# A fused H3 and MLP kernel: background work issued by an estimate of VectorE's open work instead of a fixed pace

## The chip, the cores and the metric

One core of a Trainium2 chip runs the whole program in one launch. The metric is the device time of one execution in microseconds (us). The engines are TensorE (PE in the profile, its weight loads PEld), VectorE (DVE), ScalarE (ACT), GpSimd (POOL) and SyncE (SP), which issues the DMAs.

## The reference

Two layers, each an H3 operator followed by an MLP with squared relu, on one sequence of 2048 tokens with 1024 channels; F is 3584.

```python
def _A_ref(q, k, v, shift_k, ssm_k, ssm_D):          # H3
    k_shift = sum of k_pad[:, t:t+S] * shift_k[:, 3-t]   # causal convolution over 4 tokens
    kv = k_shift * v
    y = causal convolution of kv with ssm_k over all S tokens, by channel   # written with FFTs
    return q * (y + kv * ssm_D)

def _B_ref(x, w1, b1, w2, b2):                       # MLP
    h = relu(x @ w1 + b1)
    return (h * h) @ w2 + b2

x = A_q
x = x + _A_ref(_layernorm(x), A_k, A_v, A_shift_k, A_ssm_k, A_ssm_D)
x = x + _B_ref(_layernorm(x), B_w1, B_b1, B_w2, B_b2)
x = x + _A_ref(_layernorm(x), A_k, A_v, A_shift_k, A_ssm_k, A_ssm_D)
x = x + _B_ref(_layernorm(x), B_w1, B_b1, B_w2, B_b2)
```

The convolution does not depend on the layer: the same y serves both. All arithmetic is as exact as float32: each matmul is three matmuls, of the high and low halves of its operands.

## The kernel before, in words

**Units and steps.** The tokens are four blocks of 512. A unit is one layer's MLP on one block, and `ORDER` gives the eight units: layer and block (0,0), (1,0), (0,1), (0,2), (1,1), (0,3), (1,2), (1,3). A unit is a list of steps. A step is twelve matmuls of 512 columns with one weight tile of 128 x 512: `m1` multiplies by w1, `m2` by w2. A full unit has 112 steps. Around the passage from the first unit to the second, which share a block, steps are halved (256 columns or two of four token tiles). With these the first unit has 134 steps, the second 124, the others 112: the last steps of units 0 to 4 have the numbers 133, 257, 369, 481 and 593. The loop over the steps writes the instructions of all engines in one order; each engine then runs its own in order and waits on semaphores.

**Weights.** Each weight tile is loaded (`w_load`), its high half is cast on ScalarE (`w_hi`, L770) and its low half made on VectorE (`w_lo`, L778: `whl`). In the first unit all tiles pass this way, and about two thirds are stored as pairs (`w_store`, L786, `wd_m`) and loaded ready-made in later units (`whl<-wd_m`, L768). The results of `m1` pass relu and square on ScalarE (L1141 to L1144) and give `rh`, and `rl` on VectorE (L1149). VectorE adds the results of `m2` to `acc` (L1155).

**The convolution.** Block 0 is done in a prologue (`first_block`), laid out by a planner. For blocks 1 to 3 (`sb`) it is background work, written between the steps:

- Two streams of forward transforms, by block and channel tile of 128 (`ch`, eight per block). `fwd_x` (stream x) loads k and v, does the short convolution on VectorE (L300, L302), transposes (L347), makes high and low halves (L310, L312), multiplies by the tables on TensorE (L270 to L272, tile `pt`), combines (L329, L330, L334) and stores to `xd` (L339). `fwd_g` (stream g) does the like for the filter (L370, L387 to L392, L406, L407), and stores to `gd` (L413). Each is a generator: one call goes to its next `yield`. A channel tile takes 18 calls in x and 21 in g, and more if it has to wait for a bank of `pt` (two banks, `take` and `give`, `hold`).
- The products, `prod_stream`: for each half tile and each of three pairs it loads `cx` and `cg` (L517, L519), multiplies on GpSimd two calls later (L443), reduces on VectorE four calls after the load (L447), and then finishes (`fin`: sums and butterfly on GpSimd, halves L470 and L477, inverse matmuls, L492, store to `yd`). A call returns how much it did, in thousands of elements: 43.0 for block 1, 67.6 for block 2, 92.2 for block 3, 202.8 in all. If the transforms of its channel tile are not yet done (`fwd_done`), it returns None.

**The pace before.** Each step adds a rate to `owed`, and product calls are made until at most 1.06 of the rate is spent. The rate is the work up to a unit divided by the steps left, 0.44 a step in units 0 to 2 and 0.50 in units 3 and 4. It is cut to a fifth in the last 18 steps of a unit that prepares another block, and to a tenth in half steps. Beside it both transform streams get 1.4 calls a step in units 0 to 2 and 1.1 in 3 to 5, none in those last 18 steps or in half steps, and one more in each step in which products return None. `close_conv` issues all that is left of a block's convolution at once, 18 steps before the end of the unit ahead of its first use. In those 18 steps `prep_b` prepares the next block: it adds the H3 result, normalizes (L591, L592), transposes (L649), and makes `xh` and `xl` (L657, L659), four token tiles one after the other.

Of the kernel before, what the change touches and what calls it, by code (L numbers as in the profile page):

```python
# [21 lines left out]
NT = T // P  # L22
# [8 lines left out]
CG = 64  # L31
# [13 lines left out]
AHEAD_0 = 4  # L45
BURST = 1.06
FIN = "GGG"
PACE_SLACK = {1: 74, 3: 10}
PACE_TO = {1: 2}
AHEAD_F = (6, 5)  # L50
# [4 lines left out]
WLO = {"b": "GGGV", "x": "GV"}  # L55
PREP_PACE = 0.2
FWD_RATE = {0: 1.4, 1: 1.4, 2: 1.4, 3: 1.1, 4: 1.1, 5: 1}


class Later:  # L60
# [12 lines left out]
    def flush(self):  # L73
        while self.due:
            self.tick()


# [107 lines left out]
def tile_h3_mlp(ctx: ExitStack, tc: tile.TileContext, q, kT, vT, shk, ssmT, ssmD, w1, b1, w2, b2,  # L185
                fwd_t, pro_t, inv_t, sgn_t, out):
    nc = tc.nc
    V, A, G, PE, SY = nc.vector, nc.scalar, nc.gpsimd, nc.tensor, nc.sync
    ENG = {"V": V, "G": G}
# [59 lines left out]

    held, turn, slot = [False, False], [0], {}  # L250

# [22 lines left out]
    def hold(n):  # L274
        got = take(n)
        while not got:
            yield
            got = take(n)
        return got
# [146 lines left out]

    streams = [fwd_stream("x", fwd_x), fwd_stream("g", fwd_g)]

    def fwd_tick():
        for g in streams:  # L430
            next(g, None)

    done = set()

    plag, slag = Later(), Later()

    def prod_stream():
# [11 lines left out]
        def fin(st, sm, sb, g, k):  # L449
# [31 lines left out]
            elif k == 4:  # L481
                got = take(1)
                if not got:
# [6 lines left out]
            elif k == 5:  # L490
                yo = st["yo"] = row()
                A.activation(yo["t"].rearrange("p (j e c) -> p e j c", j=BT, e=2),  # L492
                             st["b"].rearrange("p (e j c) -> p e j c", e=2, j=BT), AF.Copy, scale=1.0 / BL)
                give(st["b"])
                slag.at(1, fin, st, sm, sb, g, 6)
            else:
                SY.dma_start(YD[sb][:, :, (g - 1) * CG:(g + 1) * CG], st["yo"]["t"].rearrange("p (t c) -> p t c", t=NT))
                drop(st["yo"])
                if g == NG - 1:
                    done.add(sb)  # L500

        for sb in range(1, NB):
            nb = BT * sb + BT
            for ch in range(KT):
                while (sb, ch) not in fwd_done:
                    lag.tick()
                    yield None
# [231 lines left out]
    def row():  # L739
        while len(ring) >= RAWS and "freed" not in ring[-RAWS]:  # L740
            w_hi() if ptr["lo"] == ptr["hi"] else w_lo()
        x = {"t": mw.tile([P, 512], F32, name="wr", bufs=RAWS)}
        ring.append(x)
        return x

    def drop(*xs):
        for x in xs:
            x["freed"] = now[0]
# [531 lines left out]
    work = {sb: 3 * NG * CU * 1e-3 * sum(BT * sb + jj + 1 for jj in range(BT)) for sb in range(1, NB)}  # L1280
    WIN = {sb: min(u for u in range(NU) if ORDER[u][1] == sb) for sb in range(1, NB)}
    pace = {}
    lo_u = 0
    for sb in range(1, NB):
        if WIN[sb] > lo_u:
            group = [x for x in range(sb, NB) if PACE_TO.get(x, x) == PACE_TO.get(sb, sb)]
            hi_u = WIN[group[-1]]
            total = sum(work[x] for x in group)
            n = sum(last_step[u] + 1 - start_step[u] - 19 * (1 - PREP_PACE) for u in range(lo_u, hi_u))
            for u in range(lo_u, hi_u):  # L1290
                pace[u] = total / (n - PACE_SLACK[sb])
            lo_u = hi_u
    owed = 0.0
    fowed = 0.0
    accs = []
# [5 lines left out]
    def close_conv(nb):  # L1301
        while nb not in done:
            if next(pds) is None:
                fwd_tick()

    for s, (k, u, c, a, i, tts, w) in enumerate(steps):
# [17 lines left out]
        if k == "m1":  # L1324
# [5 lines left out]
            if i == 0 and tts[0] == 0:  # L1330
                if len(tts) < NT and a == 0:
                    xbanks = 4
                    spare = []
                    while xbanks < AHEAD[u - 1]:
                        got = take(1)
                        if got:
                            spare += got
                            xbanks += 1
                        else:
                            fwd_tick()  # L1340
                            plag.tick()
                bank = ps1 if len(tts) == NT else ps2 if a < 4 else lambda: spare.pop(0)
# [36 lines left out]
        if u + 1 < NU and not direct[u]:  # L1379
# [5 lines left out]
            if left == 18:  # L1385
# [4 lines left out]
                nxt = prep_b(*ORDER[u + 1], lag)  # L1390
        busy = left <= 18 and u + 1 < NU
        rate = pace.get(u, 100) * (PREP_PACE if busy else 1.0)
        if len(tts) < NT:
            rate *= 0.1
        owed += rate
        todo = min(owed, BURST * rate)
        while todo > 0:
            x = next(pds, 0)
            if x == 0:
                owed = todo = 0  # L1400
            elif x is None:
                fwd_tick()
                todo = 0
            else:
                todo -= x
                owed -= x
        fowed += FWD_RATE.get(u, 2) * (0.0 if busy or len(tts) < NT else 1.0)
        while fowed >= 1:
            fowed -= 1
            fwd_tick()  # L1410
    lag.flush()
# [49 lines left out]
```

## Time and profile before

| | us |
|---|---|
| median of three runs | 2942.58 (2939.34 to 2944.61) |
| the profiled execution, its own time | 2937.48 |
| its span, first to last instruction | 2935.7 |
| TensorE busy | 2794.1 (95%) |
| VectorE busy | 1707.7 (58%) |
| ScalarE busy | 978.2 (33%) |
| GpSimd busy | 917.3 (31%) |

The mean granted clock of TensorE was 0.971. A group line names code line, engine, operation, output <- inputs with shapes, count, then busy us and the mean ns of one, then the idle time ahead of it and its releaser. A wait line reads: who waited <- for whom: us in total, times, longest. The slices of the page are 40 equal parts of the span, each digit a share in tenths; a row by stretches gives for each engine busy us and, in brackets, the number of instructions. Matmuls overlap and their ends are modelled, so the distance from start to start is their pace, not their duration.

### The profile page before, as it was taken

To read this page: it belongs to the slowest core of one execution; us is meant where nothing else is said; L and a number is where in the kernel's file an instruction comes from. 1 tells how busy PE (TensorE), PEld (TensorE's weight loads), DVE (VectorE), ACT (ScalarE), POOL (GpSimd) and SP (SyncE) were. 2 spreads that over 40 slices of the span, in tenths; PEclk is the share of its full clock that TensorE was granted. 3 is DMA by queue.
4 is the path that set the end of the run, shared out by engine and by line. 5 is a ranking of instruction groups with operands and counts; after the bars stand their busy time and mean duration, and the time that the engine had idled before them with its cause. 6 is when DMAs were issued, how large, how long until landed. Compare 5 with 4: busy or idle time off the path is not lost.

```text
span 2935.7 us, 36250 instructions
## 1 busy us (share of the span) xinstructions
PE 2794.1 (95%) x13104; PEld 2328.6 (79%) x13104; DVE 1707.7 (58%) x2583; ACT 978.2 (33%) x1721; POOL 917.3 (31%) x649
## 2 busy tenths in 40 slices
PE   6878889879999999999999999999999999999999
PEld 6776767668888888878888888888888888888887
DVE  7867677776877777787875774353223522252122
ACT  3234434424233423444222422343223422242222
POOL 5634365433644264433655275201000100001000
PEclk8779999989999999999999999999999999999999
DMA  6357898777988889878887778565545755475543
GB/s 205 124 177 247 290 339 282 245 284 245 335 292 298 311 287 329 271 270 322 301 311 255 282 281 316 171 222 212 203 162 175 252 197 171 159 262 162 182 143 127
DMA packets 321572, 711.76 MB, mean 242 GB/s; under 512 B 31208, under 2 KB 123504, under 8 KB 321392
## 3 DMA queue, kind: packets, MB, share of 16 engines
q1 hardware_dynamic: 321392, 709.44, 70.3%
q8 instruction: 103, 1.69, 0.2%
q14 instruction: 77, 0.63, 0.1%
HBM read 578.24 MB, written 131.07 MB: 242 GB/s over the span
## 4 chain that ended last, share of the span: by engine, by line
PE 77%; DVE 10%; DMA 7%; issue 2%; POOL 2%; ACT 1%; SPq 1%; DVEq 0%; POOLq 0%; ACTq 0%
PE p L271 24%; PE p L270 24%; PE p L272 24%; DMA cg<-gd 3%; DVE whl L778 1%; PE pt L271 1%; PE pt L272 1%; POOL cp L443 1%; PE pt L270 1%; DMA xd<-fx 1%; DVE sm L447 1%; DMA wd_m<-whl 1%; PE p L649 1%; DMA whl<-wd_m 1%; DVE fx L300 1%
## 5 line engine op out<-in xcount | busy, mean ns | idle before, releaser
L443 POOL TENSOR_TENSOR cp<-cx,cg 128x384 f32<-128x384 f32 (+5 forms) x288 | 527.7, 1848 | 749.3 <-DMA cg<-gd 587.4
L271 PE MATMUL p<-whl,rh 128*128 128x512 f32 x1792 | 713.4, 398 | 15.8 <-DVE whl L778 14.1
L270 PE MATMUL p<-whl,rh 128*128 128x512 f32 x1792 | 716.0, 400 | 2.0 <-DMA whl<-wd_m 1.9
L270 PE MATMUL p<-xh,whl 128*128 128x512 f32 (+1 forms) x1840 | 708.7, 385 | 6.0 <-ACT wr L1141 4.0
L272 PE MATMUL p<-xh,whl 128*128 128x512 f32 (+1 forms) x1840 | 706.7, 384 | 5.8 <-DVE whl L778 5.8
L272 PE MATMUL p<-whl,rl 128*128 128x512 f32 x1792 | 711.9, 397 | 0.0
L271 PE MATMUL p<-xl,whl 128*128 128x512 f32 (+1 forms) x1840 | 706.5, 384 | 0.0
L1149 DVE TENSOR_TENSOR rl<-wr,rh 128x512 fp32r<-128x512 f32 x224 | 196.5, 877 | 545.0 <-ACT rh L1144 544.8
L778 DVE TENSOR_TENSOR whl<-wr,whl 128x512 fp32r<-128x512 f32 x403 | 360.9, 900 | 171.1 <-ACT whl L770 169.5
L271 PEld LDWEIGHTS p<-whl,rh 128*128 128x128 f32 x1792 | 341.2, 190 | 96.3 <-DVE whl L778 17.7
L770 ACT CAST whl<-wr 128x512 fp32r<-128x512 f32 x410 | 251.7, 618 | 469.5 <-PE p L272 363.5
L272 PEld LDWEIGHTS p<-xh,whl 128*128 128x128 f32 x1840 | 348.5, 189 | 74.5 <-DVE whl L778 6.2
L270 PEld LDWEIGHTS p<-xh,whl 128*128 128x128 f32 x1840 | 349.3, 190 | 72.8 <-ACT wr L1141 4.2
L270 PEld LDWEIGHTS p<-whl,rh 128*128 128x128 f32 x1792 | 341.1, 190 | 80.1 <-DMA whl<-wd_m 2.3
L272 PEld LDWEIGHTS p<-whl,rl 128*128 128x128 f32 x1792 | 340.7, 190 | 80.0
L271 PEld LDWEIGHTS p<-xl,whl 128*128 128x128 f32 x1840 | 349.0, 190 | 65.8 <-DVE xl L1068 0.3
L1141 ACT ACTIVATE wr<-p,b1t 128x512 f32<-128x512 f32 x222 | 153.2, 690 | 699.4 <-PE p L272 693.2
L1269 POOL TENSOR_TENSOR acc<-acc,px 128x1024 f32<-128x1024 f32 x32 | 86.2, 2726 | 788.4 <-DMA px<-b 773.3
L1155 DVE TENSOR_TENSOR acc<-p,acc 128x512 f32<-128x512 f32 x248 | 166.8, 688 | 250.2 <-PE p L272 249.4
L447 DVE TENSOR_REDUCE sm<-cp 128x128 f32<-128x384 f32 (+5 forms) x288 | 249.8, 875 | 92.8 <-POOL cp L443 92.8
L1142 ACT ACTIVATE wr<-wr 128x512 f32<-128x512 f32 x224 | 141.8, 633 | 7.1
L1144 ACT CAST rh<-wr 128x512 fp32r<-128x512 f32 x224 | 139.2, 621 | 7.1
(200 smaller groups left out, 2556.6 us busy)
## 6 DMA issues: line engine op xcount, KB each, us to landing
whl<-wd_m SPq DMA_DIRECT2D x500, 512.0 KB, 4.3
wr<-w SPq DMA_DIRECT2D x418, 256.0 KB, 4.7
wd_m<-whl SPq DMA_DIRECT2D x70, 512.0 KB, 6.1
cx<-xd SPq DMA_DIRECT2D x48, 512.0 KB, 5.9
cg<-gd SPq DMA_DIRECT2D x48, 512.0 KB, 5.9
gd<-fg SPq DMA_DIRECT2D x72, 256.0 KB, 6.7
cx<-xd SPq DMA_DIRECT2D x48, 384.0 KB, 5.2
cg<-gd SPq DMA_DIRECT2D x48, 384.0 KB, 6.5
```

The costliest lines, as they stand in the source:

```text
L270: PE.matmul(o, lh, rh, start=start, stop=False)
L271: PE.matmul(o, lh, rl, start=False, stop=False)
L272: PE.matmul(o, ll, rh, start=False, stop=stop)
L443: G.tensor_mul(pr.rearrange("p c i -> p i c"), xt[:, 0:j + 1], gt[:, j::-1])
L447: V.tensor_reduce(sm[:, ty, jj], st["pr"], axis=AX.X, op=OP.add)
L770: A.copy(t[:, 0], raws[n]["t"])
L778: ENG[e[n % len(e)]].tensor_sub(t[:, 1], raws[n]["t"], t[:, 0].bitcast(F32))
L1141: A.activation(r, st["o"], AF.Relu, bias=b1t[:, st["f"]:st["f"] + 1])
L1142: A.activation(r, r, AF.Square)
L1144: A.copy(st["hi"], r)
L1149: V.tensor_sub(st["lo"], st["r"]["t"], st["hi"].bitcast(F32))
L1155: V.tensor_add(accs[tt][:, d], o, accs[tt][:, d])
```

## The change

`Meter` wraps VectorE: each instruction adds an estimate of its time to `V.q`, and each step takes the step's time off. The fixed rates go. At each step `rates` gives, for x, g and products, the work still to do up to each deadline by the steps left to it (the deadlines are 18 steps before the end of units 1, 2 and 4, steps 239, 351 and 575, less a margin of 24 and, for the streams, 20 more; a channel tile is counted as 25 calls). The kind that is furthest behind, in steps, is called next, at most twice a step each, as long as VectorE's estimate is at most `ROOM` and the kind is at most `EARLY` steps ahead; a kind that is `CAP` steps behind is called whatever the estimate. The last 18 steps of a unit have no pace of their own any more. With `LEAD`, the products of a channel tile wait for the transforms of the next one too. Stores to `yd` are put in a list, from which they can be taken early, and while the second unit's spare banks are sought nobody else gets one (`closed`).

```diff
-BURST = 1.06
-PACE_SLACK = {1: 74, 3: 10}
-PACE_TO = {1: 2}
+LOCK = 1.2
+STEP_T = 2.75
+FILL = 1.0
+ROOM = 3.0
+CAP = 5
+EARLY = 40
+BURST = {"x": 2, "g": 2, "p": 2}
+TICKS = {"x": 25, "g": 25}
+MARGIN = 24
+TAIL = 20
+LEAD = 1
-PREP_PACE = 0.2
-FWD_RATE = {0: 1.4, 1: 1.4, 2: 1.4, 3: 1.1, 4: 1.1, 5: 1}
+class Meter:
+    def __init__(self, eng):
+        self.eng, self.q = eng, 0.0
+    def run(self, t):
+        self.q = max(self.q - t, 0.0)
+    def __getattr__(self, op):
+        f = getattr(self.eng, op)
+        def go(out, *args, **kw):
+            aps = [x for x in args if isinstance(x, bass.AP)]
+            src = aps[0] if op in ("tensor_reduce", "bn_stats") else out
+            n = math.prod(src.shape[1:])
+            both = len([x for x in aps if math.prod(x.shape[1:]) == n]) > 1
+            inside = any(x.tensor.name.startswith(("pt_", "p1_", "p2_")) for x in (out, *aps))
+            self.q += (0.15 + 1.04e-3 * n) * (LOCK if both and not inside else 1)
+            return f(out, *args, **kw)
+        return go
...
-                while (sb, ch) not in fwd_done:
+                while (sb, min(ch + LEAD, KT - 1)) not in fwd_done:
                     lag.tick()
                     yield None
...
+    limit = {sb: last_step[min(u for u in range(NU) if ORDER[u][1] == sb) - 1] - 18 for sb in range(1, NB)}
+    spent = dict.fromkeys("xgp", 0.0)
+    owed = dict.fromkeys("xgp", 0.0)
+    def rates(s):
+        out = {}
+        for k in "xgp":
+            total, out[k] = 0.0, 0.2
+            for sb in range(1, NB):
+                total += work[sb] if k == "p" else KT * TICKS[k]
+                left = limit[sb] - MARGIN - s - (0 if k == "p" else TAIL)
+                if left > 0:
+                    out[k] = max(out[k], (total - spent[k]) / left)
+        return out
...
-                    while xbanks < AHEAD[u - 1]:
-                        got = take(1)
-                        if got:
-                            spare += got
-                            xbanks += 1
-                        else:
-                            fwd_tick()
-                            plag.tick()
+                    spare = take(AHEAD[u - 1] - 4)
+                    closed[0] = True
+                    while not spare:
+                        fwd_tick()
+                        plag.tick()
+                        spare = take(AHEAD[u - 1] - 4)
+                    closed[0] = False
...
-        busy = left <= 18 and u + 1 < NU
-        rate = pace.get(u, 100) * (PREP_PACE if busy else 1.0)
-        if len(tts) < NT:
-            rate *= 0.1
-        owed += rate
-        todo = min(owed, BURST * rate)
-        while todo > 0:
...
-        fowed += FWD_RATE.get(u, 2) * (0.0 if busy or len(tts) < NT else 1.0)
-        while fowed >= 1:
-            fowed -= 1
-            fwd_tick()
+        V.run(STEP_T * FILL * len(tts) / NT)
+        share = 0.1 if len(tts) < NT else 1.0
+        rate = rates(s)
+        left = {k: BURST[k] if share == 1.0 else 1 for k in rate}
+        for k in rate:
+            owed[k] = min(owed[k] + share * rate[k], CAP * rate[k])
...
+        while left:
+            k = max(left, key=lambda k: owed[k] / rate[k])
+            behind = owed[k] / rate[k]
+            if behind < CAP and (V.q > ROOM or behind < -EARLY or share < 1 and behind < 0):
+                break
+            x = next(pds if k == "p" else streams[k], 0)
+            left[k] -= 1
+            if x is None and k != "p":
+                x = 1
+            if x:
+                owed[k] -= x
+                spent[k] += x
+            if not x or not left[k]:
+                del left[k]
```

## The prediction

> **What bounds the kernel now.** I read the page first, then the stretches of the span, then the waits of TensorE, VectorE and GpSimd in the stretch that loses time, then its chain of waits.
>
> ```profile
> span 2935.7 us, 36250 instructions
> PE   6878889879999999999999999999999999999999
> DVE  7867677776877777787875774353223522252122
> PEclk8779999989999999999999999999999999999999
> ```
>
> TensorE (PE) is full from the tenth slice on; VectorE (DVE) is near 75% up to two thirds of the span and then falls, because there is no background work left. The same in numbers, by stretches (columns: TensorE, its weight loads, VectorE, ScalarE, GpSimd busy us; granted clock; share of the DMA engines; GB/s):
>
> ```profile
> 250.00:600.00 350.00, 295.80 (x1329) 242.24 (x1328) 256.65 (x391) 131.96 (x245) 164.71 (x145) 0.92 0.86 290
> 600.00:700.00 100.00, 84.47 (x493) 73.70 (x492) 72.94 (x120) 35.71 (x63) 44.52 (x29) 0.91 0.68 234
> 700.00:1000.00 300.00, 298.40 (x1411) 247.92 (x1410) 227.23 (x351) 107.69 (x195) 124.43 (x88) 1.00 0.88 301
> 1000.00:1900.00 900.00, 890.24 (x4105) 736.32 (x4104) 633.22 (x829) 305.61 (x538) 425.53 (x248) 1.00 0.82 288
> 1900.00:2900.00 1000.00, 1000.00 (x4408) 820.64 (x4408) 321.90 (x557) 303.89 (x497) 33.31 (x12) 1.00 0.56 190
> ```
>
> What TensorE loses: 350 - 295.8 = 54.2 us idle in 250 to 600, and 295.8 x 0.08 = 23.7 us in a lower clock; 15.5 and 84.5 x 0.09 = 7.6 in 600 to 700; 1.6 + 9.8 = 11.4 idle in 700 to 1900 at full clock; nothing after. So all that any order of the background can win is 78 + 23 + 11 = 112 us; the prologue before 250 is not touched. Matmuls of the MLP alone, twelve to a full step:
>
> ```profile
> 250.00:600.00 350.00, 261.21 (x1049) 0.92 0.86 290
> 720.00:960.00 240.00, 220.09 (x950) 1.00 0.89 307
> 2050.00:2150.00 100.00, 100.00 (x436) 1.00 0.59 199
> ```
>
> That is 1049/12 = 87.4 steps of 4.00 us in the first stretch, 79.2 steps of 3.03 us in the second, and 36.3 steps of 2.75 us where nothing but the MLP runs. The first unit pays 1.25 us a step over the bare step. At full clock its TensorE work would be 295.8 x 0.92 / 87.4 = 3.11 us a step, transforms included.
>
> Who holds TensorE there, 250 to 700 (four rows), and 700 to 1900 (the last two):
>
> ```profile
> PE pt L347 <- DVE fg L407: 25.8, 4, 9.3
> PE p L271 <- DVE whl L778: 12.4, 5, 3.5
> PE pt L270 <- DVE fx L312: 7.5, 2, 5.8
> PE pt L271 <- DVE fg L370: 5.2, 1, 5.2
> ...
> PE pt L271 <- DVE fx L312: 2.8, 1, 2.8
> ...
> PE p L270 <- DMA whl<-wd_m: 1.9, 1, 1.9
> ```
>
> VectorE, nearly always; and mostly the background's own matmuls (pt: transposes and transforms) wait, which stand in TensorE's queue ahead of the MLP. Yet VectorE is busy only 256.65/350 = 73%, 2.94 us of each 4.00 us step. What stops it, and what stops that (250 to 700):
>
> ```profile
> DVE sm L447 <- POOL cp L443: 67.3, 23, 9.0
> POOL cp L443 <- DMA cg<-gd: 150.1, 28, 17.8
> ```
>
> The chain of waits shows one turn of it (start, us, what):
>
> ```profile
> 304.23 3.62 DMA xd<-fx
> ...
> 308.31 4.01 DMA cg<-gd
> ...
> 316.75 7.71 DMA cg<-gd
> ...
> 324.62 1.19 POOL cp L443
> ...
> 326.30 1.30 DVE fx L300
> ...
> 335.62 1.10 PE pt L347 x4
> ```
>
> A transform is stored (xd), the product of that same channel tile is let go at once and loads what has just been stored (cg), GpSimd multiplies, and the reduce (L447) stands in VectorE's in-order queue waiting for it, with everything the MLP and the next transform need behind it. Then VectorE works off the pile and TensorE waits.
>
> **The change, part by part.**
>
> *One tile further behind (LEAD).* Products of tile c start when the transforms of c+1 are done. Nothing is computed more or less. The first load of a tile then reads what was stored a whole tile earlier (7 tiles in 350 us is 50 us each; L312 ran seven times there), so the 3.62 us of the store leave the chain; the load of 4 to 7.7 us stays, and from issue to reduce there are four product calls. Of the 67.3 us I leave a third, 22, between 0 (all loads early) and 67 (loads late because the DMA engines are full).
>
> *VectorE's meter and the gate.* Each VectorE instruction adds an estimate, each full step takes off 2.75 us; a call of background is made only while the open estimate is at most 3 us, or when it is five steps behind. How true is the estimate? It charges 0.15 + 1.04 ns x 512 = 0.68 us, times 1.2 for two SBUF inputs. By the 22 groups of VectorE in 250 to 600, the first and the last of them
>
> ```profile
> L778 DVE TENSOR_TENSOR whl<-wr,whl 128x512 fp32r<-128x512 f32 x91 | 80.3, 888 | 6.4 <-ACT whl L770 5.7 <-PE pt L272 0.7
> ...
> L312 DVE TENSOR_TENSOR fx<-pt,fx 128x512 fp32r<-128x512 f32 x7 | 4.7, 677 | 0.0
> ...
> L1189 DVE TENSOR_TENSOR acc<-p,acc 128x512 f32<-128x512 f32 x1 | 0.7, 674 | 0.0
> ```
>
> the meter would have charged 267 us (91 x 0.82 = 74.5 for the first, 0.68 for the last), against 256.65 really occupied (instructions overlap by some 0.07 us). So 2.75 metered is 2.75 x 256.65/267 = 2.65 us real: the gate lets VectorE have 2.65 us a step in the first unit where it had 2.94. Of the 267, the MLP's own (91 + 22 two-input operations, 24 evictions) are 109, 1.25 a step; 1.50 are left for background, where 1.81 were issued, 17% less. What is not issued comes later, where VectorE is 75% full.
>
> *The rates.* From step 8: both transform streams (400 - 0)/(351 - 24 - 20 - 8) = 1.34 calls a step, products 202.8/(575 - 24 - 8) = 0.37. Before, 1.4 for the transforms and one more in each step in which products wait for them, and 0.44. With 18 and 21 calls a tile and 7 tiles in 87.4 steps, the old streams ran near 1.7. At the meter's prices the new rates cost 0.46 + 0.40 + 0.65 = 1.51 a step, just what the gate leaves; so no deadline is in danger in the first unit, and the second, with fewer weights to split, has room.
>
> *The sum for 250 to 600.* VectorE: 2.65 + waits. Its 93.3 us idle are 67.3 for products (22 kept) and 26 others (kept): 48/87.4 = 0.55, so 3.20 us a step. TensorE, with 17% fewer transforms: 3.05. DMA:
>
> ```profile
> 360.00:380.00 20.00, 14.15 (x59) 10.92 (x58) 10.91 (x17) 6.19 (x12) 7.75 (x6) 0.96 1.00 342
> ```
>
> A full DMA moves 342 GB/s; a step now moves 290 GB/s x 4.00 = 1.16 MB, which is 3.39 us with the old background. Some half of it are weights and stores of their halves (256 KB a step and about as much for the halves kept); with 17% off the rest it is 1.06 MB, 3.10 us. So VectorE sets the pace at 3.20, and TensorE would lose 0.15 x 87.4 = 13 us instead of 78. Against that stands that waits come in bursts which the meter cannot see (it counts VectorE's work, not its waits). I take 24 lost, gain **54**; bounds 40 (DMA at the old bytes: (4.00 - 3.39) x 87.4 = 53, less 13 for bursts) and 70.
>
> Part of this is the clock:
>
> ```profile
> 520.68 1.10 PE L347 MATMUL pt<-ident,fx 128*128 128x128 f32 x4 [9.30 <-DVE fg L407]
> ...
> 522.01 0.63 PE L271 MATMUL p<-whl,rh 128*128 128x512 f32 x1
> 522.43 0.63 PE L272 MATMUL p<-whl,rl 128*128 128x512 f32 x1
> ...
> 525.50 0.39 PE L271 MATMUL p<-whl,rh 128*128 128x512 f32 x1
> 525.73 0.39 PE L272 MATMUL p<-whl,rl 128*128 128x512 f32 x1
> ```
>
> After a wait of 9.30 us the matmuls follow every 0.42 us, then every 0.23. I let the clock's 24 us shrink with the idle time, two thirds. The Trainium skill ("TensorE: Matmul & The Clock Gate", Part 1) says that the clock halves only after an idle window of about 3.4 us; by it, waits held to some 3 us by the gate would cost no clock at all, and the gain would be 8 us more. In 700 to 1900, where the longest wait quoted is 2.8 us, the mean clock is 1.00, which agrees.
>
> *The half steps from the first unit to the second (600 to 700).* Background is held at a tenth as before; the new code asks for both spare banks at once and bars the streams meanwhile. Of the 23 us lost I take half as won, **12** (bounds 0 and 18).
>
> *The last 18 steps of a unit.* Before, background ran there at a fifth and transforms not at all; now only the gate protects them. At the end of the second unit:
>
> ```profile
> 956.33 0.73 ACT L592 ACTIVATE wr<-wr,rs 128x512 f32<-128x512 f32 x1
> 957.68 0.49 PE L649 MATMUL p<-ident,wr 128*128 128x128 f32 x3
> ```
>
> The normalized tile was ready at 957.06, 0.6 us ahead of its transposes. With up to 3 us open on VectorE the first tile comes about 2.5 us late; the wait then realigns the engines. Three such ends have background (the fourth comes after it is done): **-8** (bounds -24, four late tiles each of 2 us, and 0).
>
> *Fuller VectorE in 700 to 1900.* Background may run up to 40 steps ahead, so 17% more of the first unit's and some of the later ones' falls here, at 75% load and a DMA share of 0.82 to 0.88. VectorE at 2.65 us a step stays under the 3.03 of the step. **-5** (bounds -40 and +8 of the 11.4 lost now).
>
> A rule that speaks against filling VectorE, rows first:
>
> ```profile
> 943.16 1.85 POOL L443 TENSOR_TENSOR cp<-cx,cg 128x768 f32<-128x768 f32 x1
> 943.45 2.10 DVE L1149 TENSOR_TENSOR rl<-wr,rh 128x512 fp32r<-128x512 f32 x1 [3.29 <-ACT rh L1144]
> 949.87 0.69 DVE L1149 TENSOR_TENSOR rl<-wr,rh 128x512 fp32r<-128x512 f32 x1
> ```
>
> The same VectorE operation takes 2.10 us beside a GpSimd multiply and 0.69 alone. The Trainium skill ("GPSIMD Engine Reference", section 8, Key points) gives contention of the two engines for SBUF where VectorE reads two SBUF inputs. GpSimd's share in the first stretch is 164.7/350 = 47%, and with 83% of the products in 3.28 x 87.4 = 286 us it is 48%: no term.
>
> Net: 54 + 12 - 8 - 5 = 53 us. The profiled execution took 2937.48 us, 5.1 under the median of three; I take the gain from the median: 2942.6 - 53 = **2890 us**.
>
> **The rivals.**
>
> *A standing backlog (slower).* The gate aims at up to 3 us of open VectorE work plus the last call, in every step until the products end, where VectorE was often idle before. Each channel tile has four points where TensorE waits for VectorE (transposes, two transforms, inverse), 96 in 24 tiles, two calls behind VectorE's operation, which at two calls a step is one step, 2.75 us. If real backlog there is 3.75 us on the mean, each costs 1 us: 96 us, against 66 won and 8 at the unit ends: 2942.6 + 38 = 2981. It decides from a backlog of 2.75 + 58/96 = 3.35 us upwards. For it: the meter misses VectorE's waits, and L312 was late by up to 5.8 us. Against: in 700 to 1900 at 75% load one such wait of L312 shows.
>
> *The DMA engines bind.* If background bytes a step do not fall, the first stretch gains 40, the second unit at 0.88 and with transforms running ahead loses 15 for late weights: 40 + 8 - 8 - 15 = 25, 2918. For it: windows at 1.00. Against: TensorE waited for one weight load in all of 700 to 1900, 1.9 us.
>
> *Nearly all comes back.* 70 + 18 + 8 - 0 = 96: 2847.
>
> *The edit does nothing.* If reduces still wait for GpSimd and the gate rarely closes, the old stalls remain: 2940.
>
> **How the numbers follow.** Forecast (2865 to 2905) 0.48; DMA 0.20; nearly all 0.08; nothing 0.05; backlog 0.19, which includes a late deadline that dumps one tile's work at a unit's end. About 0.2% (6 us) is what a measurement of this kernel can tell from no change. Faster: 0.48 + 0.20 + 0.08 less 0.01 = 0.75; same 0.05; slower 0.20. The range goes from 2843 to 2968: it leaves out half of the backlog's chance and a little below. The likeliest case's own range is 2865 to 2905.
>
> **What would show it.** Right: in 250 to 600 TensorE over 90% busy and a clock of 0.97 or more, VectorE's wait L447 <- L443 near 22 us, steps of 3.2 to 3.4 us; PE pt L347 <- DVE L407 nearly gone; transforms' last stores later or at the same step. Wrong: many PE waits of 1 to 3 us on pt spread over 700 to 1900 (backlog), PE waits on whl<-wd_m or DMA share at 1.0 (DMA), waits at L649 at the unit ends above 8 us, or a burst of products just before a unit's last 18 steps.

## The result, and the profile after

The change made the kernel 1.1% slower: 2974.55 us median (2968.93 to 2977.11) against 2943.57, a ratio of 1.0106 (95% interval 1.0089 to 1.0122). 2890 was forecast, and 2974.55 is above the range (2843 to 2968). The profiled execution took 2977.11 us. A later experiment, the old pace with one small edit, takes 2878.74 us, 0.9781 (0.9762 to 0.9799), and points at what both kernels lacked.

In the kernel after, the reducing line L447 and all other VectorE operations appear as L103 (the meter's wrapper); the tile names tell them apart (`sm<-cp` is the products' reduce). GpSimd's multiply is L473 (was L443), the unit-end transposes L685 (was L649). The page first:

```profile
span 2975.3 us, 36258 instructions
...
PE   6879999899899988989899999999999999999999
...
DVE  7866777757689777997854664344223522252122
...
PEclk8779999999999999999999999999999999999999
```

The fourth to ninth slices, where TensorE lost time, are now full but for one 8. The loss has come back in slices eleven to twenty, where five 8s stand among the 9s and before there was 9 throughout. In the stretches that the prediction used (columns: TensorE, its weight loads, VectorE, ScalarE, GpSimd; granted clock; DMA share; GB/s):

```profile
250.00:600.00 350.00, 328.74 (x1579) 273.42 (x1578) 246.98 (x395) 139.69 (x254) 123.46 (x96) 0.98 0.83 285
600.00:700.00 100.00, 95.95 (x505) 81.87 (x505) 63.79 (x111) 36.20 (x65) 36.29 (x33) 1.00 0.85 278
700.00:1000.00 300.00, 278.48 (x1299) 229.86 (x1298) 239.39 (x353) 114.94 (x212) 147.37 (x111) 0.98 0.88 301
1000.00:1900.00 900.00, 841.15 (x3811) 691.41 (x3810) 628.40 (x815) 280.72 (x500) 444.58 (x262) 0.97 0.79 279
1900.00:2900.00 1000.00, 999.73 (x4411) 820.20 (x4410) 330.59 (x566) 300.60 (x494) 42.19 (x18) 1.00 0.56 191
```

From 250 to 700 TensorE now loses 21.3 + 4.0 = 25.3 us idle and 328.74 x 0.02 = 6.6 by the clock: 32 where it lost 101. From 700 to 1900 it loses 21.5 + 58.9 = 80.4 idle and 5.6 + 25.2 = 31 by the clock: 111 where it lost 11. Won 69, lost 100; the prologue, 1.3 us idler and at a clock of 0.79 instead of 0.82, gives up about 7 more. That is +38, against the +39.6 us of the spans; the clock has only two digits, so each of these clock terms is good to a few us.

Who waits for whom from 700 to 1500: VectorE's wait for products before (only its fifth row: its first was 53.3 us for ScalarE's `rh`), VectorE's two first rows after, then TensorE's first four after.

```profile
DVE sm L447 <- POOL cp L443: 14.8, 6, 4.8
```

```profile
DVE sm L103 <- POOL cp L473: 89.5, 34, 10.5
DVE rl L103 <- ACT rh L1183: 16.9, 10, 4.6
```

```profile
PE p L685 <- ACT wr L628: 16.1, 6, 10.4
PE pt L376 <- DVE fg L103: 10.9, 4, 3.5
PE pt L299 <- ACT fx L352: 10.8, 2, 8.7
PE p L299 <- DMA whl<-wd_m: 9.9, 4, 3.5
```

The wait that the first unit showed before (67.3 us from 250 to 700) now stands in the second and third units: from 700 to 1500, VectorE waits 74.7 us more for products. The two stretches beside each other, before and after:

```profile
700.00:1500.00 800.00, 789.34 (x3720) 655.69 (x3719) 614.98 (x872) 285.26 (x512) 365.07 (x231) 1.00 0.88 304
```

```profile
700.00:1500.00 800.00, 720.30 (x3320) 592.72 (x3319) 644.21 (x864) 272.75 (x500) 435.35 (x284) 0.96 0.85 294
```

TensorE stands 79.7 us instead of 10.7, 69 more. VectorE is busy 644 of 800 us instead of 615: 156 us are still free, and over half of that is the wait. One turn of it, from the timeline of after (start, us, engine, line, what, idle time before and its releaser):

```profile
1091.17 0.52 SPq L555 DMA_DIRECT2D cg<-gd  x1
...
1098.97 1.54 POOL L473 TENSOR_TENSOR cp<-cx,cg 128x640 f32<-128x640 f32 x1 [4.07 <-DMA cg<-gd]
...
1100.54 0.82 DVE L103 TENSOR_REDUCE sm<-cp 128x128 f32<-128x640 f32 x1 [4.65 <-POOL cp L473]
1101.22 0.41 ACT L500 CAST yh<-sm 128x256 fp32r<-128x256 f32 x1 [17.14 <-POOL sm L574]
...
1102.46 1.78 DVE L103 TENSOR_TENSOR yl<-sm,yh 128x256 fp32r<-128x256 f32 x1 [0.19 <-ACT yh L500]
...
1104.23 0.58 ACT L352 COPY fx<-pt 128x512 f32<-128x512 f32 x1
...
1104.86 0.58 PE L299 MATMUL pt<-yh,ih 128*128 128x256 f32 x1 [8.74 <-ACT fx L352]
```

From the issue of the load to the end of the multiply pass 9.34 us (1091.17 to 1100.51). The reduce came up in VectorE's queue before that, VectorE stood 4.65 us with everything else behind it, and TensorE stood 8.74 us. Between the two lies ScalarE: it had stood 17.14 us for GpSimd's sums of products (`yh`), and the copy (L352) that released TensorE was queued behind that. From 700 to 1500 this wait of ScalarE took 46.8 us before and 128.3 after.

### The profile page after: what moved, and what is told of

Its sections match the earlier page's. It is cut to its first block, busy times and chain, and to the rows that moved or that the text cites. A ratio compares the mean times of both kernels' runs of the same rounds, so it can differ in the third digit from the quotient of the medians.

```text
span 2975.3 us, 36258 instructions
## 1 busy us (share of the span) xinstructions
PE 2807.6 (94%) x13104; PEld 2337.0 (79%) x13104; DVE 1711.6 (58%) x2583; ACT 977.1 (33%) x1721; POOL 920.0 (31%) x649
## 4 chain that ended last, share of the span: by engine, by line
PE 67%; DVE 14%; DMA 11%; issue 3%; POOL 3%; SPq 2%; ACT 1%; DVEq 0%; POOLq 0%; ACTq 0%
PE p L299 21%; PE p L300 21%; PE p L301 21%; DMA cg<-gd 4%; DVE sm L103 2%; DMA wr<-w 2%; DVE fx L103 2%; DVE whl L103 2%; DMA whl<-wd_m 2%; POOL cp L473 2%; DVE fg L103 1%; PE pt L300 1%; PE pt L301 1%; PE pt L299 1%; DVE acc L103 1%
## 5 line engine op out<-in xcount | busy, mean ns | idle before, releaser
L473 POOL TENSOR_TENSOR cp<-cx,cg 128x384 f32<-128x384 f32 (+5 forms) x288 | 531.2, 1861 | 758.7 <-DMA cg<-gd 640.0
L103 DVE TENSOR_TENSOR rl<-wr,rh 128x512 fp32r<-128x512 f32 x224 | 196.8, 878 | 545.1 <-ACT rh L1183 545.0
L103 DVE TENSOR_TENSOR whl<-wr,whl 128x512 fp32r<-128x512 f32 x406 | 349.9, 868 | 179.0 <-ACT whl L809 170.3
L301 PEld LDWEIGHTS p<-xh,whl 128*128 128x128 f32 x1840 | 350.7, 191 | 83.2 <-DVE whl L103 14.9
L301 PEld LDWEIGHTS p<-whl,rl 128*128 128x128 f32 x1792 | 339.9, 190 | 79.7
L103 DVE TENSOR_REDUCE sm<-cp 128x128 f32<-128x384 f32 (+5 forms) x288 | 249.1, 876 | 135.2 <-POOL cp L473 134.9
L103 DVE TENSOR_TENSOR acc<-p,acc 128x512 f32<-128x512 f32 x256 | 171.0, 687 | 259.2 <-PE p L301 253.4
```

What stands on the lines that cost most here:

```text
L103: return f(out, *args, **kw)
L301: PE.matmul(o, ll, rh, start=False, stop=stop)
L473: G.tensor_mul(pr.rearrange("p c i -> p i c"), xt[:, 0:j + 1], gt[:, j::-1])
```

## The experiments

The theory after these traces: the products are a software pipeline whose distances are counted in **calls** of its generator: the multiply is written two calls behind the load, the reduce four calls behind it. The steps, the time in which load and multiply must be done, are not counted. `BURST` allows two product calls in a step, so four calls can be two steps. From 1050 to 1290 before, MLP matmuls follow thus (tile p alone):

```profile
1050.00:1290.00 240.00, 216.44 (x924) 172.32 (x923) 15.71 (x24) 12.44 (x18) 1.00 0.85 288
```

924/12 = 77 steps of 3.12 us. Two steps are 6.2 us, less than the 9.34 above; four are 12.5. In the order in which the programs are written, the old pace makes two calls in 42 of the first unit's 90 full steps (small products, of which two fit into 1.06 of the rate) and never two from the second unit on; the new code makes two in 74 of the 142 steps of the first three units that have a product call. Counted in the same way, a load's first reduce stands at most two steps behind it for 42 of the first unit's 46 loads before, and for none of the 56 in the second and third units; after the change that is so for 44 of 84 in those two units. The rivals: products read too fresh a store (LEAD); work that the gate put off makes VectorE too full later; background at the unit ends; work done too early.

| run | us, median | ratio to before (95%) | TensorE idle 250-700 | 700-1500 | reduce waits 250-700 | 700-1500 |
|---|---|---|---|---|---|---|
| before | 2943 | 1 | 69.7 | 10.7 | 67.3 | 14.8 |
| after | 2974.55 | 1.0106 (1.0089-1.0122) | 25.3 | 79.7 | 43.4 | 89.5 |
| E1 | 2936.39 | 0.9979 (0.9970-0.9988) | 74.9 | 4.1 | 52.1 | 8.4 |
| E2 | 2982.50 | 1.0134 (1.0119-1.0150) | 29.7 | 75.8 | 59.6 | 78.2 |
| E3 | 2915.50 | 0.9904 (0.9887-0.9920) | 23.1 | 40.4 | 1.8 | 24.0 |
| E4 | 2993.81 | 1.0177 (1.0160-1.0195) | 78.2 | 45.6 | 52.3 | 70.1 |
| E5 | 2964.16 | 1.0070 (1.0048-1.0093) | 23.2 | 62.3 | 14.9 | 22.4 |
| E6 | 2972.35 | 1.0118 (1.0086-1.0150) | 24.0 | 71.1 | 43.2 | 93.9 |
| E7 | 2957.21 | 1.0056 (1.0038-1.0074) | 23.8 | 67.7 | 42.3 | 76.8 |
| E8 | 2908.32 | 0.9889 (0.9859-0.9919) | 26.8 | 29.9 | 2.8 | 16.0 |
| E9 | 3015.61 | 1.0242 (1.0225-1.0259) | 35.7 | 76.7 | 83.8 | 162.2 |
| E10 | 2878.74 | 0.9781 (0.9762-0.9799) | 16.2 | 22.6 | 10.5 | 12.6 |
| E11 | 2905.05 | 0.9877 (0.9853-0.9901) | 29.4 | 22.4 | 2.5 | 8.7 |
| E12 | 2886.57 | 0.9811 (0.9794-0.9827) | 21.8 | 18.1 | - | 3.1 |
| E13 | 2882.47 | 0.9795 (0.9778-0.9811) | 18.7 | 20.0 | - | 1.7 |
| E14 | 2889.78 | 0.9825 (0.9810-0.9839) | 14.7 | 26.1 | - | 14.6 |

(Idle is the length of the stretch less TensorE's busy time. A dash: no such wait. The later stretch holds other parts of the work where the earlier one went faster, so the times decide. Idle times and waits are those of the profiled execution; in E5 that one took 2953.26, 11 us less than the median.)

**E1, LEAD alone, in the old kernel.**

```diff
-                while (sb, ch) not in fwd_done:
+                while (sb, min(ch + 1, KT - 1)) not in fwd_done:
```

> The kernel before with one edit: products of a channel tile wait for the transforms of the next tile too (LEAD = 1 under the old pace). The prediction's step (products let go at once hold VectorE on GpSimd): VectorE's wait for GpSimd's products in 250 to 700 falls from 67.3 us to 22, TensorE's idle time there from 69.7 to 45 or less, the time to 2900 to 2925 us. Rival (the gate, not LEAD, did what the new kernel wins in the first unit): idle there stays over 60, the time stays within 8 us of before.

**E2, everything but LEAD.** `LEAD = 0`.

> The changed kernel with LEAD = 0. If LEAD crowds the later units (products start late): TensorE's idle time in 700 to 1500 falls from 79.7 us to under 45, time under 2950. If it does not: idle in 700 to 1500 stays over 65 and the first unit loses some of what it won, time 2970 to 3000.

E1's wait fell from 67.3 to 52.1 us and its time by 6 us, so the rival's forecast held; taking LEAD out of the new kernel cost about 8, at the edge of what the intervals part, and left the idle time at 75.8. The freshness of the store was a small part of the old wait, and LEAD does not make the loss.

**E3, one product call a step.**

```diff
-BURST = {"x": 2, "g": 2, "p": 2}
+BURST = {"x": 2, "g": 2, "p": 1}
```

> The changed kernel with at most one product call a step instead of two. Theory bursts (two calls in a step bring a reduce within a step or two of its load, and VectorE stands waiting for GpSimd): VectorE's wait for GpSimd's products in 700 to 1500 falls from 89.5 us to under 40, TensorE's idle time there from 79.7 to under 45, time 2930 to 2945. Theory deferral (the gate left too much for units 1 and 2, VectorE has too much to do there whatever the order): idle there stays over 65, time 2965 to 2990.

59 us faster than after, and faster than either forecast. The stretch and VectorE's wait, 700 to 1500, and one of TensorE's:

```profile
700.00:1500.00 800.00, 759.57 (x3591) 631.60 (x3590) 648.89 (x902) 284.19 (x514) 443.49 (x287) 0.98 0.89 311
```

```profile
DVE sm L103 <- POOL cp L473: 24.0, 14, 7.0
```

```profile
PE pt L299 <- DVE fg L103: 20.3, 1, 20.3
```

VectorE is as busy as in after (648.89 to 644.21) while its waits fall from 89.5 to 24.0 us and TensorE's idle time from 79.7 to 40.4: in these units it is the wait that counts, not the amount of work. ScalarE's wait for the sums falls with it, from 128.3 to 51.3 us. In the second and third units 3 of 74 loads now have their reduce within two steps. Half of what TensorE still loses is a single wait of 20.3 us, which E8 removes.

**E4, the old pace for the first unit, the new scheduler from then on.** In steps below 158 the products get 0.4417 a step by the old loop, the transforms 1.4 calls; after that the new loop, with the meter at zero.

> The changed kernel with the old pace (0.44 of product work and 1.4 transform calls a step, one call more where products wait) up to the end of the half steps, and the new gate and rates from there; eight channel tiles are then transformed at the start of unit 1 instead of five. Theory deferral: TensorE's idle time in the second and third unit falls to under 25 us, the first unit loses what it lost before, time 2940 to 2960. Theory bursts: two product calls a step remain, idle in the second and third unit stays over 55, time 3000 to 3040.

The first unit is the old one again (78.2 us idle), and the second takes 432.7 us, no less than after's 420 (bias add to bias add, the table of units below), although nothing had been put off in the first. So the loss does not need deferred work. But the third unit takes 353 us, as before (358), where after took 416: what was put off does matter there. VectorE's waits for products go with the times: 58.2 us in E4's second unit and 11.9 in its third, 57.4 and 53.2 in after's. With less left to do the loop made two product calls in 11 steps of the third unit, in after in 23. The time, 2994, is neither theory's figure.

**E5, reduce one call later.**

```diff
-                            lag.at(4, red, st, sm, ty, jj)
+                            lag.at(5, red, st, sm, ty, jj)
 ...
-                                lag.at(5, fin, st, sm, sb, g, 0)
+                                lag.at(6, fin, st, sm, sb, g, 0)
```

> The changed kernel, two product calls a step as in it, but each reduce five calls after the load instead of four (the finish six). Theory bursts, by the reduce standing too close behind GpSimd: VectorE's wait for GpSimd's products in 700 to 1500 falls from 89.5 us to under 50, TensorE's idle time there from 79.7 to under 55, time under 2955. If one product a step won for another reason (two reduces in one step as a lump on VectorE): the wait falls, TensorE's idle time stays over 65, time 2965 to 2980.

The reduces' wait shrinks as forecast, the time by only 10 us, and the idle time (62.3) lies between the two forecasts. VectorE, 700 to 1500:

```profile
DVE yl L103 <- ACT yh L500: 35.7, 22, 8.6
...
DVE sm L103 <- POOL cp L473: 22.4, 15, 5.6
```

The chain behind the reduce (sums on GpSimd, `yh` on ScalarE, `yl` on VectorE) also stands calls apart, and it looks as if at two calls a step the wait goes on to its next link: 4.3 us at `yl` in after, 35.7 here.

**E6, no background in the last 18 steps of units 1 to 5.** Such steps leave the loop at once.

> The changed kernel with no background at all in the last 18 steps of units 1 to 5. Theory unit ends: TensorE's wait for the normalized tiles (L685) in 700 to 1500 falls from 16.1 us to under 3, and the second and third unit together, 836 us from add_b2 to add_b2, to 810 to 820; time 2950 to 2960. Rival: what is held there is forced into the steps behind it, L685 falls, the time stays within 8 us of 2975.

The waits at L685 go (1.2 us), but the time stays (1.0118 to 1.0106, intervals on each other): the second and third units together fall from 836 to 813 us, and the fourth rises from 327 to 346.

**E7, background at most 5 steps ahead instead of 40.** `EARLY = 5`.

> The changed kernel with EARLY = 5 instead of 40: background runs at most five steps ahead. Theory run-ahead (VectorE filled to the gate when nothing is due): TensorE's idle time in 1300 to 1500 falls from 24.6 us to under 10, time 2950 to 2965. Rival: the loss is where work is due, and idle there stays over 18, time 2970 to 2980.

17 us of the loss, as this theory forecast, though idle time from 1300 to 1500 falls only to 12.1 us; with 76.8 us of product waits and 67.7 idle left it is a part, not the main cause.

**E8, E3 and E6 together.**

> One product call a step and quiet unit ends together. If both count by themselves: the single wait of 20.3 us that the kernel with one product a step has before its second unit ends is gone, time 2885 to 2905. If what is held is only forced later: 2910 to 2920.

The 20.3 us wait is gone, and the time, 2908.32, falls between the two forecasts (E3: 2915.50; the intervals overlap).

**E9, one call a step, with distances halved.** If the distance in steps is the cause, halving it must bring the loss back although no step has two product calls.

```diff
-BURST = {"x": 2, "g": 2, "p": 2}
+BURST = {"x": 2, "g": 2, "p": 1}
 ...
-                            lag.at(2, mult, st, xt, gt, j)
-                            lag.at(4, red, st, sm, ty, jj)
+                            lag.at(1, mult, st, xt, gt, j)
+                            lag.at(2, red, st, sm, ty, jj)
 ...
-                                lag.at(5, fin, st, sm, sb, g, 0)
+                                lag.at(3, fin, st, sm, sb, g, 0)
```

> One product call a step, but the calls between load, multiply and reduce halved (multiply one call after the load, reduce two, finish three), so that in steps they stand as with two calls a step. If distance in steps is what two calls a step spoil: VectorE's wait for GpSimd's products in 700 to 1500 goes from 24.0 us (one product a step) back to over 70, time 2950 to 2985. If it is the lump of two reduces in one step: wait under 45, time under 2930.

The stretch from 700 to 1500 again, and VectorE's first wait in it:

```profile
700.00:1500.00 800.00, 723.27 (x3309) 593.97 (x3308) 592.58 (x832) 269.86 (x491) 397.29 (x268) 0.95 0.82 285
```

```profile
DVE sm L103 <- POOL cp L473: 162.2, 47, 10.2
```

It does, and more: 3015.61, 100 us behind E3 and above the forecast, with the same rules for rate, gate and limit in a step. No step has two calls, and 74 of the 77 loads of the second and third units have their reduce within two steps. This and E3 move the distance from the two sides; together they show it as the cause of most of the loss: the second and third units together take 727 us before, 836 after, 759 in E3 and 832 in E9.

**E10, the old kernel with one product call a step.** Its first unit has the same fault.

```diff
-        todo = min(owed, BURST * rate)
+        todo = min(owed, BURST * rate) if len(tts) == NT else 0
 ...
-                todo -= x
+                todo = 0
```

(No products in half steps either.)

> The kernel before, its old pace, but at most one product call a step, and none in half steps; six channel tiles are then transformed at the start of unit 1 instead of eight, with no meter and LEAD = 0. If one product a step is what wins the first unit: VectorE's wait for GpSimd's products in 250 to 700 falls from 67.3 us to under 30, the first unit from 425 us (add_b2 to add_b2) to under 385, time 2900 to 2925. If the meter's gate is: the first unit stays over 405, time 2930 to 2955.

64 us faster than before and the lowest median of all, below the forecast. Stretches, then VectorE's wait from 250 to 700:

```profile
250.00:600.00 350.00, 333.77 (x1658) 281.49 (x1657) 282.17 (x446) 149.17 (x273) 162.39 (x128) 0.97 0.89 312
600.00:700.00 100.00, 100.00 (x503) 84.64 (x502) 72.15 (x122) 37.62 (x70) 48.28 (x44) 1.00 0.93 316
```

```profile
DVE sm L447 <- POOL cp L443: 10.5, 11, 1.9
```

VectorE does more in the first stretch than before (282.17 us against 256.65), because more steps fit into it; the DMA engines move more (312 GB/s against 290), and TensorE is at 95%. The first unit is relieved, but less than in after: 68 product calls, against 91 before and 48 after, and six channel tiles transformed instead of eight and five. The second unit pays for it with 388 us instead of 369. So how much of the gain is the waits and how much the lighter load is not shown: no run has the old load without the waits. Products in half steps were taken out too; of the 53.5 us less idle time, 38.0 lie before 600. What is left is open: 22.6 us idle from 700 to 1500, of which the longest wait, 10.1 us, is for the first normalized tile at a unit's end.

**E11, E8 with the gate 15% wider** (`FILL = 1.15`).

> One product call a step, quiet unit ends, and FILL = 1.15 (the meter takes off 3.16 us a step; seven channel tiles are transformed at the start of unit 1 instead of six). If the gate at 2.75 us defers too much: the first unit keeps its 362 us within 10 and the second and third together fall from 752 us by 10 to 25, time 2885 to 2900. If the gate is what protects the first unit: it goes over 380, time 2910 to 2930.

No change within the interval (E8: 2908.32). The first unit takes 364 us, the second and third together 758 (E8: 362 and 752): neither the gain in those two nor the loss in the first came.

**E12, E8 with E5's later reduce. E13, E10 with it. E14, E13 with LEAD.**

> One product call a step, quiet unit ends, and each reduce five calls after its load. If what is left of VectorE's wait for GpSimd (16.0 us in 700 to 1500) still costs: time 2895 to 2903. If not: 2905 to 2912.

> The kernel before, its old pace, at most one product call a step and none in half steps, each reduce five calls after its load (finish six). If distance still counts at one call a step, as it did under the gate (2908 to 2887 us): VectorE's wait for GpSimd's products in 250 to 1500 falls from 23 us to under 8, time 2860 to 2875. If not: 2875 to 2885.

> The same with LEAD = 1: the same product pipeline as the gated kernel with one product call, quiet ends and a late reduce (2887 us), under the old pace. If the gate wins something beside the distances: over 2890. If it wins nothing: within 8 us of 2887. If it costs: under 2879. By the first runs LEAD is worth some 6 us, so under 2870 if e13 comes to 2875.

With one call a step the later reduce brings the new scheduler 22 us (E8 to E12), more than forecast, and the old pace nothing (E10 to E13). In the third unit, counted in the written order, 38 of 42 loads in E8 have their first reduce three steps behind them, and 27 of 28 in E10 four or more; that may be why, but was not tried by itself. E12 and E14 have the same product pipeline, one under the meter and urgency, the other under the old pace: 0.9811 and 0.9825, intervals on each other. The meter, the urgency and the gate are then worth nothing that can be measured. LEAD costs about 7 us here (E13 to E14, at the edge of what the intervals part), where it won 6 in E1; why was not settled.

The units' times, from one bias add on GpSimd (`acc<-acc,px`) to the next (the add is written 16 steps into a unit). The first unit of before, from 241.0 us on, ends at the first row, that of after, from 234.9 on, at the second:

```profile
665.72 2.40 POOL L1269 TENSOR_TENSOR acc<-acc,px 128x1024 f32<-128x1024 f32 x1 [9.38 <-DMA px<-b]
```

```profile
590.19 2.41 POOL L1308 TENSOR_TENSOR acc<-acc,px 128x1024 f32<-128x1024 f32 x1 [8.00 <-DMA px<-b]
```

| us | before | after | E3 | E4 | E9 | E10 |
|---|---|---|---|---|---|---|
| first unit | 425 | 355 | 358 | 434 | 372 | 346 |
| second | 369 | 420 | 392 | 433 | 427 | 388 |
| third | 358 | 416 | 367 | 353 | 405 | 355 |
| fourth | 326 | 327 | 347 | 313 | 352 | 334 |

## Why the prediction was wrong, point by point

**The first unit (54, and 12 in the half steps): the size right, the reason not.** 69 us came against 66. TensorE is 328.74/350 = 94% busy at a clock of 0.98, and L376 waiting for `fg` is no longer among its waits. From about 515 us on (before: 581) the first unit runs half steps; up to there, tile p alone and then everything:

```profile
250.00:515.00 265.00, 239.37 (x1009) 189.86 (x1007) 15.75 (x24) 14.45 (x21) 0.99 0.87 297
```

```profile
250.00:515.00 265.00, 256.49 (x1181) 211.47 (x1180) 188.54 (x289) 113.43 (x205) 92.90 (x80) 0.99 0.87 297
```

1009/12 = 84.1 steps of 3.15 us, where 3.2 to 3.4 were forecast. The forecast let VectorE set this pace, with 2.65 us of work a step. It does only 188.54/84.1 = 2.24 us, and TensorE's own work, 256.49/84.1 = 3.05 us, nearly fills the step. So the gain came from putting off far more than the 17% of the forecast. The reduces from 250 to 600, before and after (third number pair of each row),

```profile
250.00:600.00 350.00, 0.00 (x0) 0.00 (x0) 52.50 (x88) 0.00 (x0) 111.79 (x88) 0.92 0.86 290
```

```profile
250.00:600.00 350.00, 0.00 (x0) 0.00 (x0) 28.54 (x48) 0.00 (x0) 62.73 (x48) 0.98 0.83 285
```

are 48 instead of 88. The 17% supposed that background fills the gate in every step. In the order in which the program is written, the gate stopped the loop in only 35 of the first unit's 90 full steps. In 62 of them a product call returned None, because the transforms of the next channel tile, at two calls a step at most, were not done.

The lighter load carries the gain: E2 and E9, as light, lose only 29.7 and 35.7 us from 250 to 700 with product waits of 59.6 and 83.8; E3 has next to no waits and loses 23.1. So the waits, which the forecast wanted gone, hardly cost here once VectorE is light. E10 gets there with more background, 2.64 us of VectorE a full step (before 3.00, after 2.24), and next to no waits. The load was one cure, and the one whose bill came later.

**LEAD (67.3 to 22): the figure met, its reason only in part.** From 250 to 600, the stretch that the prediction named, the wait did fall to 22:

```profile
DVE sm L103 <- POOL cp L473: 22.3, 10, 5.8
```

But that is over 48 reduces instead of 88, 0.46 us each against 0.76. LEAD alone (E1) leaves 49.0 us of the 67.3 in this stretch, and the new kernel without LEAD (E2) has 45.9, so it took both LEAD and the missing products to come to 22; that they met the figure is luck. Without LEAD, but with one product call a step (E10), 5.7 us are left. The chain quoted from before, a load of what had just been stored, was a real turn, but not what most of the 23 waits came from. That two products stood in one step was left out of the account.

**"From issue to reduce there are four product calls" is the step that hid the loss.** It took a distance in calls as a time. The text even has "at two calls a step is one step" for the transforms, in the backlog rival, but the products' own limit of two was not put beside it.

**Fuller VectorE in 700 to 1900 (-5, bounds -40 and +8): the term that failed.** It came to -100, with the unit ends in it. "VectorE at 2.65 us a step stays under the 3.03 of the step" counts work: 644 us of 800 do fit. It puts the waits at nothing: from 700 to 1500 VectorE's waits for products rose from 14.8 to 89.5 us, and TensorE's idle time with them from 10.7 to 79.7. The meter leaves them out too, as the text says of bursts in the first unit: while VectorE stands, the meter counts its work as done and lets more in. And the work put off, taken as 17%, was nearly half of the first unit's products. Busy time and product waits of VectorE together, as a share of the stretch, and TensorE's idle share:

| | before | E1 | after | E3 | E9 | E10 |
|---|---|---|---|---|---|---|
| 250-700: busy + waits | 0.73 + 0.15 | 0.74 + 0.12 | 0.69 + 0.10 | 0.72 + 0.00 | 0.68 + 0.19 | 0.79 + 0.02 |
| TensorE idle | 0.15 | 0.17 | 0.06 | 0.05 | 0.08 | 0.04 |
| 700-1500: busy + waits | 0.77 + 0.02 | 0.78 + 0.01 | 0.81 + 0.11 | 0.81 + 0.03 | 0.74 + 0.20 | 0.81 + 0.02 |
| TensorE idle | 0.01 | 0.01 | 0.10 | 0.05 | 0.10 | 0.03 |

In this table TensorE idles 0.06 to 0.17 of the stretch where the waits are 0.10 or more, and 0.01 to 0.05 where they are 0.03 or less. The sum of work and waits alone does not decide it: E8, not in the table, has 0.84 + 0.02 from 700 to 1500 and idles 0.04, and E5 has 0.80 + 0.03 and idles 0.08, with its waits at `yl`. The work alone costs little: E10 carries the 0.81 of after without the waits at 0.03. The waits alone cost as much as both: E9 has 0.74 of work, less than before, and idles 0.10.

**The unit ends (-8, bounds -24 and 0).** Inside the bounds in the wait itself (16.1 us at L685), past the 8 us named as a sign; but E6 took the wait away, and what the second and third units won the fourth lost, so it is no term of its own.

**The rates.** Transforms and products at 1.34 and 0.37 a step left five channel tiles transformed at the second unit's first full step where the old pace had eight (counted in the written order). "The second has room" was not so. E4, which starts the second unit as far on as before, loses as much in it, and nothing in the third (353 us): being late makes the loss longer, by the steps with two product calls that it asks for, but the loss also comes without it. Some of it stays when the waits are gone: in E3 the second unit still takes 392 us instead of 369, and TensorE is busy for 383.63 of them, with work that the first unit had left.

**The rivals.** The standing backlog gave 2981, 6 us from the measured time, and its signs are partly there: TensorE waits on pt of up to 8.7 us, spread over 700 to 1500. The nearness is luck, for its mechanism is not what the runs show. It had 1 us at each of 96 points from work open on VectorE; E3 and E10 have the same busy share in those units (0.81) and half and a third of the idle time. What stood ahead of the transforms was, by E3 and E9, in the main a reduce that could not start. The DMA rival fell (9.9 us on `whl<-wd_m`, share 0.85 from 700 to 1500), and so did the edit that does nothing.

**The clock.** In the first stretch it came back with the idle time (0.92 to 0.98), and was lost with it in the next (1.00 to 0.97). The Trainium skill ("TensorE: Matmul & The Clock Gate", Part 1) ties the loss to idle windows of about 3.4 us; the trace agrees in the main: longest quoted wait 2.8 us and clock 1.00 before, waits to 10.4 us and 0.97 after. It does not agree throughout: from 1040 to 1060 before, the mean clock was 0.91, and TensorE's longest wait there was 2.6 us.

## What to carry to other kernels

Distances in a software pipeline belong in the consumer's time (here steps), not in calls of the generator that issues it; where two calls can fall into one step, the distance is half of what the code seems to say. A reduce that waits on an in-order engine holds up all that is queued behind it, so look for its wait before you look for load. A meter that counts an engine's work and not its waits lets more in just when the engine stands; a meter with the waits in it was not tried here, and a fixed pace with the same distances did as well (E14). A lighter stretch is a loan: what is put off meets the next stretch, and the waits that it brings count there.

## What the runs showed of the hardware

The prediction gave contention between VectorE and GpSimd no term, since GpSimd's share hardly changed in the first unit. (Its "3.28 x 87.4 = 286 us" does not follow from the 54 us won, which leave 296; GpSimd's share would be 46% instead of 48, and nothing else changes.) From 700 to 1500 GpSimd's busy time went from 365.07 to 435.35 us of 800. At a unit's end in after, VectorE, and the multiplies of GpSimd at that time:

```profile
1315.73 5.31 POOL L473 TENSOR_TENSOR cp<-cx,cg 128x896 f32<-128x896 f32 x2
...
1318.73 2.86 DVE L103 SCALAR_TENSOR_TENSOR yt<-px,mv,yt 128x512 f32<-128x512 f32 x1
...
1322.29 0.75 DVE L103 SCALAR_TENSOR_TENSOR yt<-px,mv,yt 128x512 f32<-128x512 f32 x1
```

The first `yt` took 2.86 us and ended at 1321.59, just after GpSimd's multiplies (1321.04); the same operation took 0.75 us once they were over. How much of the loss this is was not tried by itself. But the loss does not follow GpSimd's time: from 700 to 1500 E3 has 443.49 us of GpSimd and half the idle time of after, E9 has 397.29 us and nearly all of it.
